# Cached grouped-query attention, twice: load gates in one table, first scores moved up, seven remainder tiles back from DMA

## The chip, the cores and the metric

The kernel runs on one core of a Trainium2 chip. The metric is device time in microseconds (us) of the whole program, from launch to the last store; lower is better. A core has a matrix engine (TensorE, PE in the profile, its weight loads PEld), a vector engine (VectorE, DVE), an activation engine (ScalarE, ACT), GpSimd (POOL) and SyncE (SP), which only issues transfers here. Transfers are issued from two in-order queues, that of SP and that of ACT, and run on 16 shared DMA engines. PSUM has eight banks, into which PE writes.

## The reference

Two independent problems, A and B, have the same shapes and are computed alike; their outputs stand side by side.

```python
B, Sq, D = 16, 80, 576
Hq, Hkv, Sk, Dh = 32, 16, 512, 128          # two query heads share one key/value head
q = (x @ wq).reshape(B, Sq, Hq, Dh).transpose(0, 2, 1, 3)
k = repeat(k_cache, 2, axis=1);  v = repeat(v_cache, 2, axis=1)
p = softmax(einsum("bhqd,bhkd->bhqk", q, k) * Dh ** -0.5)
o = einsum("bhqk,bhkd->bhqd", p, v)
out = o.transpose(0, 2, 1, 3).reshape(B, Sq, Hq * Dh) @ wo
```

All tensors are bf16. Per problem, K and V are 16 x 16 x 512 x 128 each (33.5 MB each), wq is 576 x 4096 and wo 4096 x 576.

## The kernel before

**Units.** The work is cut into 128 units (64 for A, then 64 for B). A unit is one batch and four key/value heads, so eight query heads. Its queries are 4 x 160 rows (two heads of 80 rows share a K/V head). Each 160 is split into 128 rows and 32 remainder rows; the four remainders are put together into one more tile of 128 rows. So a unit has five score tiles of 128 x 512, k = 0 for the remainders and k = 1 to 4 for the four heads. Eight units (eight batches) make an octet, with 16 octets `goct` in all. Octets come in fours: two column blocks `q` of wq for the first eight batches (`half` 0), and the same two for the last eight (`half` 1).

**A unit's steps**, with their lines in the kernel before: query projection (L581, five matmuls of 320 columns for each of eight heads and two batch groups, evicted to `qT` by ACT L592 or DVE L593); scores (L691 remainders, L705 heads); negative maximum (DVE L714); exponential with row sum (ACT L718); reciprocal (DVE L724); scaling of the probabilities (POOL L727); transposition of the probability tile into `pT` by four matmuls with the identity (PE L733) and a copy out of PSUM (DVE L739 for the remainder tile, L741 for a head's); product with V (PE L778), evicted to `oT` by ACT L794. Every 16 units, over both halves, an output projection (L831) is added into `acc` (ACT L843) or added to it and stored (DVE L859, SP L865).

**Remainder tiles by DMA.** In units that the table `RSEL` names, the remainder tile is not transposed on PE. SP issues a DMA transposition from `p_sb` to `pT` (L745), and there is no copy on DVE. `pT` has three slots (`NPT`), so the transposition of unit U may not be issued before the V products of unit U-3 are done. All four V products of unit U read what it brings. Before the change `RSEL` names 97 units.

**Loads.** SP issues, from one in-order queue: K of every unit by DMA transposition (L656, five slots), x of problem B by DMA transposition, five pieces for each half (L521), wq (L557, L554) and wo (L621) for later octets, the remainder transpositions and the output stores. V comes on ACT's queue (L660, four slots). x of A is loaded plainly (L487) and transposed on PE (L502). An issue of a K transposition can occupy SP for several microseconds.

**The planner.** The order of work is not written out. `_Sched.arrange` plays the program through with costs for each operation: each operation has a key (the step at which it is due; five steps are one unit), and where several are ready on an engine the smallest key less an `ahead` goes first. Each engine then runs the fixed order that comes out, with semaphore waits. So a constant in the planner changes the order of instructions, and is no wait by itself. `after` is a gate: a load isn't placed before a named V product (`S.marks`, four per unit) has started in the plan. `LA` = 13 lets the scores run 13 steps ahead of the V products; `lead` lets projections run 15 units ahead at first and `QL1` at the end (`QL2` for octet 1).

**Names that the change touches.** `XR`, `WQR`, `WOR`: gates of B's x, of wq and of wo, as a first unit and a step in units. `XLD`: keys of the four loads of A's x, two per half. `x` in the loop over `goct == 0`: keys of the first octet's projections, 16 of them: for each of the eight heads i one over two batches (c = 0, 160 columns) and one over six (c = 1, 480 columns); a unit's remainder scores need all eight heads of its batch. `RDO`, `PTO`, `OEO`, `OVO`: the `ahead` of the remainder transpositions, of the copies to `pT`, of the evictions to `oT`, and of those of the output projection. `QEO` is used nowhere. `VPH`, `VU0`: V of unit U from `VU0` on is gated `VPH` quarter units before its use. `NWARM2`: matmuls on dummy data while the second part of x is awaited.

Of the kernel before, what the change touches and what calls it, by code (L numbers as in the profile page):

```python
# [13 lines left out]
LA = 13  # L14
# [6 lines left out]
QL0 = 15.0  # L21
QL1 = 11.0
KC = 2.1
# [3 lines left out]
XC = 0.4  # L27
QL2 = 10.3
VC = 1.75
# [6 lines left out]
NWARM = 8  # L36
NWARM2 = 4
NWC = 4
# [5 lines left out]
VLAG = 2.0  # L44
VPH = 11
VU0 = 14
KPH = 27
# [13 lines left out]
RG = (((0, 1, 2, 3, 4),), ((0,), (1, 2, 3, 4)))  # L61
RSEL = ((18, 24, (1, 3)), (24, 46, (0, 1, 2, 3)), (46, 62, (1, 3)), (62, 126, (0, 1, 2, 3)))
RDC = 0.72
RDK = 2.0
RDO = 10.0
RDD = 1.2
PTO = 1.0
OEO = 4.0
OVO = 8.0
QEO = 6.0  # L70
RCO = 2.0
NSS = 6
OPSPLIT = 2
XLD = ((-100.0, -60.0), (-25.0, -24.9))
XH = 0.0
XB = 4.0
WQ1 = -16.8
WQ1B = 0.02
# [3 lines left out]
LPC = 29.0  # L82
WOR = (((4.0, 1.5), (12.0, 1.5)), ((9.0, 1.8), (16.5, 1.8)), ((9.0, 1.8), (16.5, 1.8)), ((9.0, 1.8), (16.5, 1.5)))
WQR = (2.0,3.5,9.5)
XR = (-12.0,1.6)

# [275 lines left out]
def bass_concat_heads__gqa_block_cached__gqa_block_cached__near_ridge_kernel(  # L362
# [27 lines left out]
    with ExitStack() as es:  # L390
# [123 lines left out]
        for half in range(NPP):  # L514
            x_ap = probs[1][0]
            st0 = UPR + 16 * half - lead[NG // 2 + 2 * half]
            for ck in range(5):
                def em_ldxt(e, x_ap=x_ap, half=half, ck=ck):
                    src = x_ap.rearrange("b s d -> (b s) d")[half * NROW:(half + 1) * NROW, :]
                    c0 = ck * 128 if ck < 4 else D - 128  # L520
                    return e.dma_start_transpose(xT[:, half, ck:ck + 1, :],  # L521
                                                 src[:, c0:c0 + 128].rearrange("n (c d) -> n c d", c=1))

                S.add("sp", 5.0 * st0 - 20.0 + 0.01 * ck, em_ldxt,
                      writes=[R(("xT", half, b_), 1) for b_ in range(NRT)] if ck == 0 else [R(("xT", half, "t", ck), 1)],
                      dsem="d_x%d0" % half, name="ldxt%d.%d" % (half, ck), stream="x", dur=0.7, cost=0.85, xp=True,
                      after=int(4 * (st0 + XR[0] + XR[1] * ck)))

# [4 lines left out]
        for goct in range(NG):  # L533
# [6 lines left out]
            for pi, (c0, c1) in enumerate(pieces):  # L540
# [10 lines left out]
                for j, (k0, k1, n0, n1) in enumerate(parts):  # L551
# [6 lines left out]

                    at = WQR[0] + WQR[1] * j if k0 == 0 else WQR[2]
                    S.add(eng, t_ld + 0.01 * k0 if goct < 2 else 5.0 * (sp_ + at), em_ldw,  # L560
# [6 lines left out]
            for i in range(8):  # L567
                for c in range(2):
                    if goct == 0:
                        b0, nb = ((0, 2), (2, 6))[c]  # L570
                        x = -LA - ((6.0, 3.6), (1.2, 0.5))[i // 4][c] + (0.6 if i < 4 else 0.05 if c == 0 else 1.2) * (i % 4)
                    else:
# [372 lines left out]
```

## Time and profile before

| | before |
|---|---|
| runs shown | 768.44, 772.54, 777.40 us; median 772.54 us |
| the profiled execution | 776.17 us, of which its span is 774.4 us |
| PE busy | 758.1 us, 98% of the span |
| DVE, ACT, POOL busy | 671.1 (87%), 608.7 (79%), 434.1 us (56%) |
| DMA moved | 173.26 MB, mean 224 GB/s; SP's queue q1 79.3%, ACT's queue q10 29.7% of 16 engines' span |
| K transpositions | 64 + 64, 512 KB each, 7.4 us from issue to landing (median) |
| V loads | 64 + 64, 512 KB each, 5.2 to 5.4 us |
| remainder transpositions | 97, 128 KB each, 5.0 us |

The 1.8 us between the profiled execution's time and its span lie outside what the profile shows of the program. The busy time of PE counts pipelined matmuls one behind the other; how far it is work is seen from the distance between starts (a 128-column matmul 56 ns, 160 columns 69 ns, 288 columns 123 ns, 320 columns 136 ns, 512 columns 216 ns apart where nothing waits). In the tables by stretch, the columns are the stretch, its length, and for each engine the busy time with the number of instructions in brackets, then the granted clock of PE, the DMA share and GB/s.

### The profile page before, as it was taken

To read this page: it belongs to the slowest core of one execution; us is meant where nothing else is said; L and a number is where in the kernel's file an instruction comes from. 1 tells how busy PE (TensorE), PEld (TensorE's weight loads), DVE (VectorE), ACT (ScalarE), POOL (GpSimd) and SP (SyncE) were. 2 spreads that over 40 slices of the span, in tenths; PEclk is the share of its full clock that TensorE was granted. 3 is DMA by queue.
4 is the path that set the end of the run, shared out by engine and by line. 5 is a ranking of instruction groups with operands and counts; after the bars stand their busy time and mean duration, and the time that the engine had idled before them with its cause. 6 is when DMAs were issued, how large, how long until landed. Compare 5 with 4: busy or idle time off the path is not lost.

```text
span 774.4 us, 20988 instructions
## 1 busy us (share of the span) xinstructions
PE 758.1 (98%) x7866; PEld 572.9 (74%) x7866; DVE 671.1 (87%) x1588; ACT 608.7 (79%) x1706; POOL 434.1 (56%) x647
## 2 busy tenths in 40 slices
PE   8999999999999997999999999999899999999998
PEld 4577777777777775777777777767677777777786
DVE  4999999888888987899899898988798988898982
ACT  1898988888888886787787878877688788888860
POOL 1565665656565655565655556665455565565650
PEclk9999999999999999999999999999999999999999
DMA  9999999999999999999999999999999999999931
GB/s 248 243 234 230 231 223 254 229 231 222 205 218 220 246 226 217 263 223 245 234 232 213 243 233 255 226 237 227 238 221 214 219 204 210 255 233 249 256 109 32
DMA packets 432996, 173.26 MB, mean 224 GB/s; under 512 B 329600, under 2 KB 432512, under 8 KB 432896
## 3 DMA queue, kind: packets, MB, share of 16 engines
q1 hardware_dynamic: 366208, 105.71, 79.3%
q10 hardware_dynamic: 66688, 66.20, 29.7%
q8 instruction: 64, 1.05, 0.6%
q14 instruction: 36, 0.29, 0.1%
HBM read 87.46 MB, written 2.95 MB: 117 GB/s over the span
## 4 chain that ended last, share of the span: by engine, by line
PE 96%; DMA 1%; ACT 1%; issue 1%; DVE 0%; SPq 0%
PE ps L581 23%; PE ps L831 20%; PE ps L778 19%; PE ps L733 16%; PE ps L705 14%; PE ps L691 4%; ACT p_sb L718 1%; DMA acc<-in_A_x_dram 1%; DMA pT<-p_sb 1%; PE ps L502 0%; DVE negmax L714 0%; ACT oT L794 0%; DVE qT L593 0%; SPq L487 0%; DVE osb L859 0%
## 5 line engine op out<-in xcount | busy, mean ns | idle before, releaser
L727 POOL TENSOR_SCALAR p_sb<-p_sb,rinv 128x512 bf16<-128x512 bf16 x640 | 431.7, 698 | 317.4 <-DVE rinv L724 317.2
L718 ACT ACTIVATE p_sb<-ps,negmax 128x512 bf16<-128x512 f32 x640 | 439.6, 693 | 60.1 <-DVE negmax L714 49.0
L714 DVE TENSOR_REDUCE negmax<-ps 128x1 f32<-128x512 f32 x640 | 424.4, 678 | 25.9 <-PE ps L691 13.5
L778 PE MATMUL ps<-pT,v_sb 128*128 128x160 bf16 x2048 | 220.9, 233 | 7.8 <-issue 5.2
L741 DVE COPY pT<-ps 128x512 bf16<-128x512 bf16 x512 | 207.9, 412 | 20.3 <-PE ps L733 17.8
L581 PE MATMUL ps<-xT,wq_sb 128*128 128x320 bf16 (+2 forms) x1280 | 213.7, 300 | 0.7 <-ACT p_sb L718 0.6
L733 PE MATMUL ps<-ident,p_sb 128*128 128x128 bf16 x2172 | 207.2, 219 | 0.0
L778 PEld LDWEIGHTS ps<-pT,v_sb 128*128 128x128 bf16 x2048 | 164.1, 98 | 54.0 <-issue 6.4
L705 PE MATMUL ps<-kT,qT 128*128 128x512 bf16 x512 | 193.9, 380 | 1.0 <-ACT p_sb L718 1.0
L733 PEld LDWEIGHTS ps<-ident,p_sb 128*128 128x128 bf16 x2172 | 154.9, 98 | 34.3 <-issue 5.9
L831 PE MATMUL ps<-wo_sb,oT 128*128 128x288 bf16 x1280 | 170.8, 286 | 0.0
L581 PEld LDWEIGHTS ps<-xT,wq_sb 128*128 128x128 bf16 x1280 | 116.8, 98 | 53.5 <-ACT oT L794 5.1
L794 ACT CAST oT<-ps 128x320 bf16<-128x320 f32 x256 | 109.1, 426 | 52.8 <-PE ps L778 50.0
L831 PEld LDWEIGHTS ps<-wo_sb,oT 128*128 128x128 bf16 x1280 | 122.8, 98 | 33.0 <-issue 0.8
L718 ACT ACTIVATION_READ_ACCUMULATOR p_sb<-ps,negmax 128x1 f32 x640 | 131.4, 205 | 0.0
L592 ACT ACTIVATE qT<-ps 128x320 bf16<-128x320 f32 (+1 forms) x129 | 56.0, 434 | 31.5 <-PE ps L581 31.1
L593 DVE TENSOR_SCALAR qT<-ps 128x320 bf16<-128x320 f32 (+2 forms) x127 | 61.7, 487 | 13.1 <-PE ps L581 12.1
L705 PEld LDWEIGHTS ps<-kT,qT 128*128 128x128 bf16 x512 | 50.1, 98 | 6.2 <-ACT p_sb L718 2.3
L859 DVE TENSOR_TENSOR osb<-ps,acc 128x288 bf16<-128x288 f32 x40 | 18.2, 456 | 29.1 <-PE ps L831 28.5
L691 PE MATMUL ps<-kT,qT 128*32 128x512 bf16 x512 | 40.0, 388 | 1.8 <-ACT p_sb L718 1.8
L724 DVE RECIPROCAL rinv<-rowsum 128x1 f32<-128x1 f32 (+2 forms) x225 | 36.7, 163 | 4.3 <-ACT p_sb L718 4.3
L843 ACT COPY acc<-ps 128x288 f32<-128x288 f32 x40 | 16.0, 399 | 4.2 <-PE ps L831 3.3
(19 smaller groups left out, 42.4 us busy)
## 6 DMA issues: line engine op xcount, KB each, us to landing
v_sb<-in_B_v_cache_dram ACTq DMA_DIRECT2D x64, 512.0 KB, 5.2
v_sb<-in_A_v_cache_dram ACTq DMA_DIRECT2D x60, 512.0 KB, 5.3
wo_sb<-in_A_wo_dram SPq DMA_DIRECT2D x16, 288.0 KB, 5.1
wo_sb<-in_B_wo_dram SPq DMA_DIRECT2D x16, 288.0 KB, 4.4
wq_sb<-in_B_wq_dram SPq DMA_DIRECT2D x16, 256.0 KB, 5.1
out_dram<-osb SPq DMA_DIRECT2D x40, 72.0 KB, 3.9
v_sb<-in_A_v_cache_dram SPq DMA_DIRECT2D x4, 512.0 KB, 5.4
wq_sb<-in_A_wq_dram SPq DMA_DIRECT2D x8, 256.0 KB, 5.1
```

The costliest lines, as they stand in the source:

```text
L581: last = e.matmul(ps[:, vb.phys, 0:n1 - n0], lhsT=wq_sb[:, wsl, ck, i * 128:(i + 1) * 128], rhs=xT[:, half, ck, n0:n1], start=(ck == 0), s ...
L593: return e.tensor_scalar(dst, src, SCALE, None, op0=AluOpType.mult)
L691: last = e.matmul(ps[32 * g4:32 * g4 + 32, vb_.phys, :], lhsT=qT[:, qp_, g4 * 160 + 128:g4 * 160 + 160], rhs=kT[:, ks_, :, g4 * 128:(g4 + ...
L705: return e.matmul(ps[:, vb.phys, :], lhsT=qT[:, qp, gl * 160:gl * 160 + 128], rhs=kT[:, ks, :, gl * 128:(gl + 1) * 128], start=True, stop= ...
L714: return e.tensor_reduce(negmax[:, si:si + 1], ps[:, vb.phys, :], axis=AX.X, op=AluOpType.max, negate=True)
L718: return e.activation(p_sb[:, psl, :], ps[:, vb.phys, :], AF.Exp, bias=negmax[:, si:si + 1], scale=1.0, accum_out=rowsum[:, ss, k:k + 1])
L727: return e.tensor_scalar(p_sb[:, psl, :], p_sb[:, psl, :], rinv[:, ss, k:k + 1], 1.0, op0=AluOpType.mult, op1=AluOpType.mult)
L733: last = e.transpose(psb[:, vt.phys, j * 128:(j + 1) * 128], p_sb[:, psl, j * 128:(j + 1) * 128], ident[:])
L741: return e.tensor_copy(pT[:, pts, :, 0:4, gl * 32:gl * 32 + 32], psb[:, vt.phys, 0:512].rearrange("p (j h c) -> p j h c", j=4, h=4))
L778: last = e.matmul(ps[:, vo.phys, off:off + 160], lhsT=v_sb[:, vs, gl, j * 128:(j + 1) * 128], rhs=pT[:, pts, j, :, gl * 32:gl * 32 + 32], ...
L794: return e.copy(dst, src)
L831: last = e.matmul(ps[:, vb.phys, 0:DC], lhsT=oT[:, hi, rb * 128:(rb + 1) * 128], rhs=wo_sb[:, hi, c3 * DC:(c3 + 1) * DC], start=(hi == 0), ...
```

## The change

The loads of wq, wo and B's x get gates of their own by half and by column block, so that they are spread further apart: B's first x half comes over units 36 to 40 (before 38.75 to 45), its second over 57.75 to 64.5 (before 55.25 to 61.75). The second half of A's x is loaded after the first four K tiles, not ahead of all. In the first octet, two of the eight projections over six batches come before the first scores, not four, and the other six are given keys between those of the scores. In units 78 to 91 only every second remainder tile goes by DMA, so that 90 do in all; seven more go by PE and DVE. Some priorities, V's gate (a quarter of a unit later, and from unit 10 on) and the number of dummy matmuls are changed with it. No instruction computes anything else.

```diff
-QL1 = 11.0
+QL1 = 10.5
-QL2 = 10.3
+QL2 = 10.6
-NWARM2 = 4
+NWARM2 = 2
-VPH = 11
-VU0 = 14
+VPH = 10
+VU0 = 10
-RSEL = ((18, 24, (1, 3)), (24, 46, (0, 1, 2, 3)), (46, 62, (1, 3)), (62, 126, (0, 1, 2, 3)))
+RSEL = ((18, 24, (1, 3)), (24, 46, (0, 1, 2, 3)), (46, 62, (1, 3)), (62, 78, (0, 1, 2, 3)), (78, 92, (1, 3)), (92, 126, (0, 1, 2, 3)))
-RDO = 10.0
+RDO = 6.0
-PTO = 1.0
-OEO = 4.0
-OVO = 8.0
-QEO = 6.0
+PTO = 2.0
+OEO = 8.0
+OVO = 0.0
+QEO = 0.0
-XLD = ((-100.0, -60.0), (-25.0, -24.9))
+XLD = ((-100.0, -60.0), (-8.0, -7.9))
+G0H = -2.9
+G0C = (-3.6, -3.2, 1.2, 2.7, 4.2, 5.7, 7.2, 8.2)
-WOR = (((4.0, 1.5), (12.0, 1.5)), ((9.0, 1.8), (16.5, 1.8)), ((9.0, 1.8), (16.5, 1.8)), ((9.0, 1.8), (16.5, 1.5)))
-WQR = (2.0,3.5,9.5)
-XR = (-12.0,1.6)
+WOR = (((4.0, 1.5), (12.0, 1.5)), ((9.0, 2.0), (17.0, 2.0)), ((9.0, 2.0), (17.0, 2.0)), ((9.0, 2.0), (17.0, 1.5)))
+WQR = ((2.0, 2.5, 11.0), (4.0, 2.5, 12.0))
+XR = ((-14.8, 0.9), (-10.0, 1.7))
...
-                      after=int(4 * (st0 + XR[0] + XR[1] * ck)))
+                      after=int(4 * (st0 + XR[half][0] + XR[half][1] * ck)))
...
-                    at = WQR[0] + WQR[1] * j if k0 == 0 else WQR[2]
+                    at = WQR[q % 2][0] + WQR[q % 2][1] * j if k0 == 0 else WQR[q % 2][2]
...
-                        x = -LA - ((6.0, 3.6), (1.2, 0.5))[i // 4][c] + (0.6 if i < 4 else 0.05 if c == 0 else 1.2) * (i % 4)
+                        x = -LA + (G0C[i] if c else -6.0 + 0.6 * i if i < 4 else G0H + 0.05 * (i - 4))
```

## The prediction

> **What bounds the kernel now.** I read the page first: the busy shares, the slices, the chain. Then the busy times by stretches of 20 us, SP's own timeline where PE falls short, and the chain there.
>
> ```profile
> PE 758.1 (98%) x7866; PEld 572.9 (74%) x7866; DVE 671.1 (87%) x1588; ACT 608.7 (79%) x1706; POOL 434.1 (56%) x647
> PE 96%; DMA 1%; ACT 1%; issue 1%; DVE 0%; SPq 0%
> ```
>
> PE is busy 98% of the span and carries 96% of the chain that ended last. So time is gained only by giving PE less to do or by taking away its few holes. The stretches show them:
>
> ```profile
> 0.00:20.00 20.00, 17.53 (x125) 9.95 (x126) 10.31 (x23) 3.75 (x8) 2.44 (x7) 1.00 1.02 248
> 20.00:40.00 20.00, 18.43 (x181) 11.82 (x179) 19.57 (x45) 17.07 (x48) 10.98 (x17) 1.00 1.06 251
> 40.00:60.00 20.00, 20.00 (x215) 15.04 (x213) 18.99 (x44) 18.02 (x51) 12.63 (x19) 1.00 1.14 234
> 300.00:320.00 20.00, 15.41 (x148) 11.20 (x146) 13.94 (x33) 12.95 (x36) 8.81 (x14) 0.91 1.23 219
> 500.00:520.00 20.00, 18.65 (x192) 13.66 (x190) 17.42 (x40) 16.52 (x49) 10.86 (x17) 1.00 1.16 225
> 520.00:540.00 20.00, 19.36 (x202) 14.94 (x201) 16.99 (x41) 14.60 (x42) 10.82 (x17) 1.00 1.09 234
> 540.00:560.00 20.00, 16.93 (x175) 12.46 (x173) 14.24 (x34) 13.37 (x38) 10.09 (x16) 1.00 1.08 230
> ```
>
> PE, the first busy time, is full from 40 us to the end, apart from two places: 300 to 320 us (4.59 us short, and its clock mean only 0.91) and 500 to 560 us (1.35, 0.64 and 3.07 us short). The start is the third place. What ends the holes is seen in the timelines of SP and PE and, for the later place, in the chain (start, length, what):
>
> ```profile
> 297.66 3.34 SPq L656 DMA_TRANSPOSE kT<-in_A_k_cache_dram  x1
> 301.10 1.22 SPq L745 DMA_TRANSPOSE pT<-p_sb  x1
> 307.76 0.44 PE L778 MATMUL ps<-pT,v_sb 128*128 128x160 bf16 x4 [4.59 <-issue]
> ...
> 541.96 4.84 DMA pT<-p_sb
> 546.85 0.45 PE ps L778 x4
> ```
>
> PE's first hole ends at the V product of unit 49. The waits call this one "issue", but by the landing records that unit's remainder transposition, issued at 301.10, landed at 307.67. Its slot had been free since 292.72, the end of unit 46's last V product. So it stood 8.4 us behind other issues, of which the K transposition from 297.66 was the last, and left the V product 0.09 us of slack. I made the same three numbers for all 97 transpositions. From unit 24 to 44 the lag is 0 to 2.6 us and the slack 6 to 11 us. It then rises to 11.5 us at unit 51, and again from 2.2 us at unit 80 to 9 at unit 84 and 12 at unit 90; units 49, 84, 86, 87 and 89 have slack under 0.25 us, and those are the holes. A lag of about 8.4 us is where PE begins to pay.
>
> **The change, part by part.** The sum goes against the profiled execution: 776.17 us, that is 774.4 of span and 1.8 around it. It lies 3.6 us above the median of the runs shown, whose holes I take to be smaller by about that.
>
> (1) *The holes, and their price.* PE short 4.59 + 1.35 + 0.64 + 3.07 = 9.65 us. The first one also costs clock: the clock records give half speed from 308.4 to 311.8 us, which loses 1.7 us. Together 11.35 us. The shorter holes left the clock at 1.00.
>
> (2) *Do the new gates empty the queue there?* I added up the bytes whose gate lies in a span of units (K and V 1.05 MB a unit, remainder 0.131, wo piece 0.295, wq piece 0.262 and 0.131, x piece 0.164). Units 41 to 50: 14 loads before, 9 after; 13.8 MB against 12.75. At 10 units of 5.6 us less what the hole takes, about 50 us, that is 275 against 255 GB/s, where the stretches with a backlog moved 219 to 250. Units 36 to 41 take up what was moved: 3 loads before, 7 after, 6.5 against 7.2 MB in 28.7 us, 226 against 252 GB/s. Measured lag before grew by 10 us where my excess makes 6, so I scale by 1.7: after the change about 1.5 us at unit 41 and 5 to 6 at unit 50, under 8.4. Units 78 to 84: before 8.75, after 8.2 MB (three remainders fewer); units 84 to 90: 8.3 against 7.9. A lag of 4 to 5 us instead of 9 to 12. Units 84 and 86 have no transposition left to wait for. So both places clear, by 3 us of lag. I leave 1.5 us for small waits: **-9.85 us**. Ends: all 11.35 gone, or half (5.7).
>
> (3) *Seven remainder tiles on PE.* 7 x 4 matmuls x 56 ns = **+1.57 us**, all on the path, since PE is full there. Seven copies of 410 ns (L739) are 2.9 us of DVE, beside PE: DVE has 1.5 to 3 us free in each 20 us from 500 on and 1.15 from 480 to 500; there two copies use 0.8 of it. SP loses seven issues of 1.2 us.
>
> (4) *The start.* PE runs without a hole from 8.27 to the first scores:
>
> ```profile
> 8.27 7.99 PE L581 MATMUL ps<-xT,wq_sb 128*128 128x160 bf16 x65
> 16.19 0.40 PE L691 MATMUL ps<-kT,qT 128*32 128x512 bf16 x4
> 17.59 0.69 ACT L718 ACTIVATE p_sb<-ps,negmax 128x512 bf16<-128x512 f32 x1 [3.04 <-DVE negmax L714]
> 23.22 0.39 PE L705 MATMUL ps<-kT,qT 128*128 128x512 bf16 x1 [0.40 <-ACT p_sb L718]
> ```
>
> Two projections of five 480-column matmuls (1.01 us each) leave the road to the first scores: they come 2.0 us earlier. They need the second wq piece (landed 11.5 us) and K of unit 0 (12.94); both gain from two x loads leaving the queue ahead of them. From 20 to 31 us PE has holes of 0.3 to 0.7 us because ACT frees score banks too slowly (the last line); an earlier start of ACT fills them with the projections put off. What limits it: DVE is 19.57 of 20 busy from 20 to 40 us, and K of unit 5 landed at 35.23 for scores at 37.09, a slack of 1.86 that bytes, not order, decide. So the gain is at most 2.5 and I take **-1.5 us**. The other side: the second half of A's x, landed at 8.8 and 11.4 us before, now comes behind K of unit 3 and, by the K and V landings (25.18, 27.82, 29.21), at about 24 and 28 us. PE transposed it from 26.8 to 32 us, so up to 1 us earlier would now wait; at worst +1.5. The Trainium skill's "DMA: Bandwidth & Descriptors", section "Rules for kernel authors", says to issue a transfer early and wait for it late, which speaks against this move; by it the start would lose that 1.5 us and the sum be 769.4; no row of before can show it.
>
> (5) *V's gate* is a quarter unit, 1.1 to 1.6 us, later. V's slack at its product is 4 us and more except at units 15, 82 and 83 (2.8, 3.1, 2.5 us), so 0; with cover gone, some 1 us at each. *Dummy matmuls*: two fewer (0.43 us) lie in a wait for x (1.2 us), 0. *Priorities*: an op eviction that waits behind one exponential (0.69 us) holds one of the two banks that projections share with V products; PE has other work ready, 0, bounds -1 and +2. *RDO* lets a wq issue (0.58 us) go ahead of a remainder; beside 3 us of room, 0. *Lead* of projections: 0, the same matmuls.
>
> Sum: 776.17 - 9.85 + 1.57 - 1.5 = **766.4 us**, 0.8% under the median. One per cent (7.7 us: 764.8 and 780.3) is about what a measurement of this kernel tells from no change, for its runs spread by 9 us.
>
> **Rivals.**
> - *Everything clears* (chance 0.25): no hole is left and the start gives its full 2.5: 776.17 - 11.35 + 1.57 - 2.5 = 763.9. For it: at units 62 to 78 and 92 to 126, with every remainder by DMA, no wait of PE shows. Against it: DVE's 19.57.
> - *Half the holes stay* (0.2): the loads are moved and no byte but 0.92 MB is saved; 252 GB/s at units 36 to 41 already exceeds what backlogged stretches moved. 776.17 - 5.7 + 1.57 = 772.0, no change against the median.
> - *Remainders late all over* (0.1, slower): with `RDO` 6 each wq, wo or K that is ready passes a remainder in SP's order, and with five x pieces in under four units, at a place where every unit has one, the lag passes 8.4 us before unit 46. The two old places keep their holes and a third of the first one's price (4.59 + 1.7) is added; 776.17 + 6.3 + 1.57 - 1.5 = 782.5. Against it: lag 0 to 1.1 us at units 34 to 43 before, with two x pieces among them.
> - *The forecast* (0.45).
>
> The range goes from just under the first rival to above the third case, whose small start loss it takes in: 763 to 775. Faster by over 1%: the first rival and a sixth of the forecast, 0.32; slower 0.1; within 1% 0.58.
>
> **What would show it.** PE full in 300 to 320 and 500 to 560 us with clock 1.00; remainder transpositions issued within 6 us of their slot's release at units 45 to 55 and 80 to 92; first remainder scores near 14 us; L733 x2200. Wrong if a hole of over 2 us stands before a V product (L778), or if PE waits between 24 and 33 us for the transposition of x (L502), or if a stretch after 40 us falls short with DVE over 19.5.

## The result

| | before | after |
|---|---|---|
| median of 20 runs | 773.92 us (766.92 to 793.91) | 779.15 us (773.05 to 785.67) |
| ratio to before, 95% interval | 1 | 1.0102 [1.0071, 1.0132] |
| profiled execution, its span | 776.17, 774.4 us | 776.12, 774.4 us |
| PE's work at full rate | 738.0 us | 739.1 us |
| PE's loss against it | 32.3 us | 31.1 us |

The forecast was 766.4 us, 0.8% faster; by the ratio the changed kernel is 1.0% slower. The two profiled executions take the same time, so the traces tell what was traded, and only the comparisons tell which way the sum leans. Ratios are taken over runs within 1.5% of the fastest run of the same kernel, here 18 of 20 against 14 of 20, so a ratio can differ from the quotient of two medians (1.007 here). *Work* and *loss* come from the distances between the starts of neighbouring matmuls: the work is the distance where nothing waits (56 ns for 128 columns and so on), the loss is the rest. About 0.4 us in each 20 us of loss is there in every stretch.

The page of the changed kernel: the busy line, the chain's shares by engine, and the group of the transpositions on PE.

```profile
PE 759.6 (98%) x7892; PEld 573.3 (74%) x7892; DVE 677.6 (88%) x1594; ACT 607.2 (78%) x1700; POOL 434.1 (56%) x647
PE 86%; DMA 6%; DVE 5%; SPq 2%; ACT 1%; issue 0%; ACTq 0%
L735 PE MATMUL ps<-ident,p_sb 128*128 128x128 bf16 x2200 | 209.1, 219 | 0.3 <-DVE pT L743 0.2
```

PE is as full as before, with 28 more transposition matmuls. The chain is another: 6% of it is now DMA (1% before) and 2% SP's queue. (The 5% of DVE stand for no hole: the chain of `e_light`, below, has 4% and PE is full.) The stretches of the changed kernel, columns as before:

```profile
0.00:20.00 20.00, 16.21 (x112) 9.17 (x113) 9.29 (x22) 4.61 (x10) 2.44 (x7) 1.00 1.03 217
20.00:40.00 20.00, 19.78 (x188) 12.95 (x186) 18.85 (x41) 16.26 (x46) 10.12 (x15) 1.00 1.12 249
300.00:320.00 20.00, 18.65 (x198) 13.64 (x196) 18.58 (x45) 16.36 (x45) 12.19 (x19) 1.00 1.21 248
340.00:360.00 20.00, 17.62 (x190) 13.30 (x188) 15.63 (x38) 13.41 (x39) 10.91 (x17) 1.00 1.08 248
460.00:480.00 20.00, 18.77 (x200) 14.16 (x198) 16.74 (x39) 15.42 (x43) 11.17 (x17) 1.00 1.16 250
500.00:520.00 20.00, 20.00 (x209) 15.09 (x207) 17.85 (x42) 16.75 (x49) 12.72 (x20) 1.00 1.12 241
520.00:540.00 20.00, 20.00 (x211) 15.60 (x210) 17.63 (x43) 15.75 (x43) 10.94 (x17) 1.00 1.04 247
540.00:560.00 20.00, 20.00 (x214) 14.98 (x213) 17.41 (x42) 17.25 (x49) 12.76 (x20) 1.00 1.25 195
720.00:740.00 20.00, 18.89 (x203) 14.38 (x201) 18.11 (x44) 15.96 (x45) 12.44 (x20) 1.00 1.13 227
```

Three of these stretches had been full in the kernel before:

```profile
340.00:360.00 20.00, 20.00 (x210) 15.34 (x209) 17.92 (x43) 16.22 (x45) 11.69 (x18) 1.00 1.22 246
460.00:480.00 20.00, 20.00 (x213) 15.26 (x211) 17.93 (x44) 16.92 (x48) 13.17 (x20) 1.00 1.14 234
720.00:740.00 20.00, 20.00 (x221) 15.52 (x218) 19.49 (x48) 17.07 (x48) 13.37 (x21) 1.00 1.10 233
```

The holes that the prediction wanted filled are nearly filled: 500 to 560 us is full, and 300 to 320 us is 1.35 us short at clock 1.00, where it was 4.59 short at 0.91. New holes stand elsewhere. In loss of PE, half clock included:

| stretch | before | after | difference |
|---|---|---|---|
| 300 to 320 and 500 to 560 us | 13.25 | 3.50 | -9.75 |
| 340 to 360 | 0.42 | 2.95 | +2.53 |
| 440 to 500 | 1.28 | 4.06 | +2.78 |
| 560 to 580 | 0.20 | 1.28 | +1.08 |
| 720 to 740 | 0.41 | 1.65 | +1.24 |
| 0 to 40 (start) | 6.31 | 7.11 | +0.80 |
| the rest | 10.45 | 10.59 | +0.14 |

Together -1.18 us; with 1.13 us more work (seven remainder tiles 1.57, two dummy matmuls -0.43) that is -0.05 us, the difference of the two profiled times. So 7.8 us of holes at new places, after 40 us, have eaten most of what the old places gave. But the profiled execution of before lies 2.3 us over the median of its runs, and that of after 3 us under: a mean run of the changed kernel loses 3.6 us at half clock (mean granted clock 0.995 over 20 runs), its profiled execution none between 6.9 and 774.9 us.

What ends the largest new hole is read from the chain of the changed kernel (start, length, what):

```profile
347.34 4.03 SPq L658
351.37 0.05 issue
351.42 5.19 DMA wo_sb<-in_A_wo_dram
356.61 0.14 issue
356.74 2.12 PE ps L833 x16
```

The last piece of wo for the output projection was issued at 351.42, behind a K transposition whose issue held SP for 4 us, landed at 356.61, and the projection (L833) started 0.13 us later. In the kernel before the same piece had landed 7.64 us before it was wanted. PE's waits in the changed kernel (for what, us in total, times, longest) put this wait first:

```profile
PE ps L833 <- DMA wo_sb<-in_A_wo_dram: 2.8, 2, 2.4
PE ps L780 <- DMA pT<-p_sb: 2.4, 3, 1.2
PE ps L504 <- DMA acc<-in_A_x_dram: 1.8, 1, 1.8
```

The second line is the remainders, whose transpositions are still late at unit 49 and newly at 51, 73, 76 and 92 (slack 0.13 us each). Their lag behind the release of their slot, which the prediction saw falling to 4 to 6 us, has a mean of 3.2 us over all units (2.9 before), and 21 units have over 6 us (16 before). At units 73, 76 and 92 the lag was only 3.3, 4.5 and 4.6 us; there the transfer itself was slow, 7.8 to 8.6 us from issue to landing against a median of 5.1.

### The profile page after: what moved, and what is told of

The parts are those of the page before. It is cut to its first block, busy times and chain, and to the rows that moved or that the text cites. A ratio compares the mean times of both kernels' runs of the same rounds, so it can differ in the third digit from the quotient of the medians.

```text
span 774.4 us, 21004 instructions
## 1 busy us (share of the span) xinstructions
PE 759.6 (98%) x7892; PEld 573.3 (74%) x7892; DVE 677.6 (88%) x1594; ACT 607.2 (78%) x1700; POOL 434.1 (56%) x647
## 2 busy tenths in 40 slices
DMA packets 429188, 172.34 MB, mean 223 GB/s; under 512 B 325792, under 2 KB 428704, under 8 KB 429088
## 3 DMA queue, kind: packets, MB, share of 16 engines
HBM read 87.46 MB, written 2.95 MB: 117 GB/s over the span
## 4 chain that ended last, share of the span: by engine, by line
PE 86%; DMA 6%; DVE 5%; SPq 2%; ACT 1%; issue 0%; ACTq 0%
PE ps L583 20%; PE ps L833 19%; PE ps L780 16%; PE ps L735 14%; PE ps L707 13%; PE ps L693 4%; DMA pT<-p_sb 3%; DVE negmax L716 3%; SPq L658 2%; DMA wo_sb<-in_A_wo_dram 1%; DVE pT L743 1%; DMA wq_sb<-in_A_wq_dram 1%; ACT p_sb L720 0%; DVE pT L741 0%; SPq L559 0%
## 5 line engine op out<-in xcount | busy, mean ns | idle before, releaser
L716 DVE TENSOR_REDUCE negmax<-ps 128x1 f32<-128x512 f32 x640 | 423.5, 680 | 22.3 <-PE ps L707 11.6
L735 PEld LDWEIGHTS ps<-ident,p_sb 128*128 128x128 bf16 x2200 | 156.5, 98 | 37.3 <-DVE pT L743 5.9
L833 PE MATMUL ps<-wo_sb,oT 128*128 128x288 bf16 x1280 | 171.0, 286 | 2.8 <-DMA wo_sb<-in_A_wo_dram 2.8
L833 PEld LDWEIGHTS ps<-wo_sb,oT 128*128 128x128 bf16 x1280 | 122.5, 98 | 38.9 <-DVE rinv L726 2.6
L594 ACT ACTIVATE qT<-ps 128x320 bf16<-128x320 f32 (+2 forms) x123 | 53.8, 437 | 33.4 <-PE ps L583 32.3
L595 DVE TENSOR_SCALAR qT<-ps 128x320 bf16<-128x320 f32 (+2 forms) x133 | 64.6, 486 | 14.3 <-PE ps L583 12.5
```

The lines of the kernel that those rows point to most:

```text
L595: return e.tensor_scalar(dst, src, SCALE, None, op0=AluOpType.mult)
L716: return e.tensor_reduce(negmax[:, si:si + 1], ps[:, vb.phys, :], axis=AX.X, op=AluOpType.max, negate=True)
L735: last = e.transpose(psb[:, vt.phys, j * 128:(j + 1) * 128], p_sb[:, psl, j * 128:(j + 1) * 128], ident[:])
L833: last = e.matmul(ps[:, vb.phys, 0:DC], lhsT=oT[:, hi, rb * 128:(rb + 1) * 128], rhs=wo_sb[:, hi, c3 * DC:(c3 + 1) * DC], start=(hi == 0), ...
```

## Experiments

Three theories stood at first: the **gates** (new places for the loads make other loads late), the **start** (the first scores are not earlier), and the **remainder tiles** (seven more on PE). Later came the **wo wait** and the **priorities**. "Undone" means the changed kernel with the values of before; "alone" means the kernel before with the new values.

| kernel | what | median (range), us | before beside it | ratio [95%] |
|---|---|---|---|---|
| `after2` | the change again | 775.74 (766.94 to 785.09) | 773.40 | 1.0032 [0.9988, 1.0075] |
| `e_light` | the change, lighter wq and wo loads | 767.86 (766.66 to 773.30) | 773.40 | 0.9973 [0.9935, 1.0011] |
| `u_gates` | gates of x, wq, wo undone | 772.95 (769.20 to 782.45) | 772.82 | 1.0007 [0.9975, 1.0039] |
| `u_x` | gates of x undone | 773.56 (770.69 to 779.85) | 777.62 | 1.0008 [0.9968, 1.0049] |
| `u_w` | gates of wq, wo undone | 772.05 (768.07 to 781.50) | 777.62 | 0.9965 [0.9922, 1.0009] |
| `u_w2` | `u_w` again | 774.83 (767.90 to 783.74) | 773.41 | 1.0037 [0.9999, 1.0075] |
| `u_gv` | all gates and V's undone | 780.15 (772.39 to 798.52) | 777.62 | 1.0079 [1.0030, 1.0127] |
| `d_gates` | gates of x, wq, wo alone | 784.01 (772.21 to 792.26) | 777.62 | 1.0062 [1.0003, 1.0122] |
| `u_vgate` | V's gate undone | 776.81 (770.09 to 786.23) | 772.82 | 1.0049 [1.0017, 1.0082] |
| `u_rsel` | 97 remainders by DMA | 778.44 (772.24 to 795.85) | 772.82 | 1.0075 [1.0028, 1.0122] |
| `d_rsel` | 90 remainders, alone | 773.55 (766.24 to 783.22) | 773.40 | 1.0007 [0.9963, 1.0050] |
| `d_xr` | x gates and 90 remainders, alone | 771.80 (766.45 to 778.42) | 773.41 | 0.9987 [0.9946, 1.0027] |
| `u_start` | start undone | 782.23 (766.74 to 795.75) | 772.82 | 0.9999 [0.9934, 1.0063] |
| `u_ws` | gates of wq, wo and x loads of the start undone | 774.17 (770.33 to 781.49) | 773.40 | 1.0029 [0.9991, 1.0067] |
| `u_wo` | gates of wo undone | 775.10 (769.15 to 784.11) | 773.41 | 1.0025 [0.9989, 1.0061] |
| `x_wo` | gates of wo later still | 776.82 (769.12 to 783.28) | 773.41 | 1.0058 [1.0023, 1.0094] |
| `u_pri` | the five priorities undone | 773.33 (768.60 to 782.02) | 776.05 | 0.9998 [0.9953, 1.0044] |
| `d_pri` | the five priorities alone | 778.34 (774.77 to 785.91) | 776.05 | 1.0110 [1.0026, 1.0194] |

### The change again

No edit; it tells how far one comparison carries.

> The changed kernel once more, on the same chip as the next three. 0.4 to 1.0% over the kernel before; if it is level with it here, the loss lies within what chips differ by and the load gates are not its cause.

It came out 0.3% slower, with an interval that takes in no change, against 1.0% in the first comparison; the intervals overlap only from 0.71 to 0.75%. So the forecast gain of 0.8% is ruled out, the cost is put at 0.3 to 1.0%, and a difference of 0.7% between two of the kernels below, compared at different times, is not to be read by itself. The trace has the wait for wo at the same place, longer, and this time it costs clock as well (stretches of `after2`):

```profile
340.00:360.00 20.00, 16.96 (x180) 12.60 (x178) 16.07 (x38) 14.02 (x41) 12.73 (x19) 0.96 1.22 234
360.00:380.00 20.00, 20.00 (x189) 14.93 (x188) 15.54 (x37) 11.37 (x33) 7.38 (x11) 0.87 1.01 198
```

PE's gap before the output projection is 3.20 us, and the clock is at half from 358.3 to 365.1 us: 3.4 us more. One wait of this kind, 6.6 us in all, is 0.85% of the run.

Of the new holes of the first trace, this is the only one that the second repeats: the loss is 1.28 us at 440 to 500 us, 0.43 at 560 to 580 and 0.59 at 720 to 740, as before the change or near it, and only 6 remainders lag over 6 us (21 in the first trace). The sum does repeat: the two old places give 10.1 us, 8.1 us are lost at other places after 40 us (6.0 of it at 340 to 380 us) and 1.0 more at the start. So a part of the places in one trace is chance, and that something is lost elsewhere is not.

### Is it the load on the DMA engines?

```diff
+                        if wv > 1:
+                            return e.dma_start(wq_sb[:, wsl, k0:k0 + 1, n0:n1], src[0:128, :].rearrange("(c p) n -> p c n", p=128))
...
+                    if sg:
+                        return e.dma_start(wo_sb[:, wc * hc:wc * hc + 1, c3 * DC:(c3 + 1) * DC],
+                                           src[0:128, :].rearrange("(h p) n -> p h n", p=128))
```

> The changed kernel, but of every later wq and wo piece (third weight block on) only a quarter of its rows is loaded: 10 MB of 173 less, with the same issues at the same places; the rest of the weights is stale, so the output is another. If late remainder transpositions and K tiles behind a full queue make all of PE's holes after the start: holes gone between units 36 and 110, lag under 3 us, 764 to 767 us and runs within 6 us. If the order of the issues on SP (one behind a K that blocks) makes them and not the bytes: 773 us or more.

Of every later wq and wo piece only a quarter is loaded, so that the kernel leaves out a part of the weights and its output is another. With 10 of 172 MB less and every instruction kept, the holes go. Stretches of `e_light`:

```profile
300.00:320.00 20.00, 20.00 (x214) 14.98 (x212) 19.84 (x47) 17.43 (x49) 12.65 (x19) 1.00 1.07 236
340.00:360.00 20.00, 20.00 (x216) 15.32 (x209) 18.09 (x44) 14.47 (x41) 10.12 (x16) 1.00 0.96 201
500.00:520.00 20.00, 20.00 (x216) 15.11 (x215) 17.50 (x42) 16.43 (x47) 11.59 (x18) 1.00 1.00 201
540.00:560.00 20.00, 20.00 (x212) 15.53 (x214) 16.70 (x40) 16.64 (x49) 12.28 (x19) 1.00 0.99 200
```

PE is full at the DMA's 200 to 236 GB/s, where the changed kernel moves 195 to 248 there. No remainder lags over 6 us (mean 0.9), and after 40 us no hole is over 0.4 us. Its median is 7.9 us under that of `after2` on the same chip. So the holes of the changed kernel are loads that come late because too much is to be moved, and those 10 MB decide. The same kernel's runs spread over 6.6 us, those of `after2` over 18: the spread, too, is mostly made by the transfers. The kernel before was not run with the lighter loads, so this tells what makes the holes, and not what makes the changed kernel slower than the kernel before.

### The gates

`u_gates` (`u_x` has the second line alone, `u_w` and `u_w2` the first and third):

```diff
-WOR = (((4.0, 1.5), (12.0, 1.5)), ((9.0, 2.0), (17.0, 2.0)), ((9.0, 2.0), (17.0, 2.0)), ((9.0, 2.0), (17.0, 1.5)))
+WOR = (((4.0, 1.5), (12.0, 1.5)), ((9.0, 1.8), (16.5, 1.8)), ((9.0, 1.8), (16.5, 1.8)), ((9.0, 1.8), (16.5, 1.5)))
-XR = ((-14.8, 0.9), (-10.0, 1.7))
+XR = ((-12.0, 1.6), (-12.0, 1.6))
-WQR = ((2.0, 2.5, 11.0), (4.0, 2.5, 12.0))
+WQR = ((2.0, 3.5, 9.5), (2.0, 3.5, 9.5))
```

> The changed kernel with the load gates of before (B's x, wq, wo). Theory G: the backlog at units 64 to 82 goes (lag of the remainder transpositions there back to 0 to 3 us from 4 to 8), the one at 45 to 57 stays; 773 to 775 us. Theory V and theory S: the lag at 64 to 82 stays 4 us or more, and the time 778 us or more.

> The changed kernel with only the gates of B's x as before. All engines but SP keep their order; on SP the ten x pieces move. Theory Gx, that five x pieces in four units, where every unit has a remainder transposition, start the backlog: 773 to 775 us, and the slack of the remainder transpositions at units 41 to 45 back from a mean of 3.7 to 6 us or more. Theory Gw, that the wq and wo pieces, now issued in pairs behind one K, do it: 778 to 780, slack at 41 to 45 under 5 us.

> The changed kernel with only the gates of wq and wo as before. Theory Gw: 773 to 775 us. Theory Gx: 778 to 780 us, slack at units 41 to 45 under 5 us.

> Once more the changed kernel with the wq and wo gates of before, whose first result was 0.4% under the kernel before with an interval that takes in no change. If that was real: 0.2 to 0.6% faster again. If chance: level or slower.

With the gates of before, all or a part of them, the changed kernel is level with the kernel before. The lag that was expected to go with `u_gates` didn't: at units 64 to 82 its mean is 5.5 us (5.4 in the changed kernel). That `u_w` seemed 0.35% faster is not borne out: the second comparison of the same kernel gives 0.4% slower. In its second trace there is no hole at unit 49, but one of 5.21 us at 150 us, where K is late, and one of 1.67 at 532: the queue falls behind somewhere, and not always in the same place.

The hole at unit 49 follows the gates as predicted. With the old gates of x, wq and wo it is 4.76 us (before), 4.79 (`d_rsel`), 4.29 (`u_gates`), 3.38 (`u_gv`) and more in `d_pri` (below); with the new ones 1.02 (after), 1.17 (`after2`), 1.27 (`u_start`), 1.29 (`u_rsel`), and there is none in `u_vgate`, `u_pri` and `d_gates`. That piece of the mechanism is shown.

```diff
 # u_gv: the three lines of u_gates, and
-VPH = 10
-VU0 = 10
+VPH = 11
+VU0 = 14
```

> The changed kernel with the load gates and V's gate as before; new start, 90 remainders by DMA and priorities stay. If the two gates are all that costs: 768 to 771 us, under the kernel before, with no hole of over 3 us in the units 78 to 92. If V's gate does nothing beside the load gates: 772 to 774, as with the load gates alone undone.

```diff
 # d_gates: the kernel before with
+WOR = (((4.0, 1.5), (12.0, 1.5)), ((9.0, 2.0), (17.0, 2.0)), ((9.0, 2.0), (17.0, 2.0)), ((9.0, 2.0), (17.0, 1.5)))
+WQR = ((2.0, 2.5, 11.0), (4.0, 2.5, 12.0))
+XR = ((-14.8, 0.9), (-10.0, 1.7))
```

> The kernel before with only the new load gates (B's x, wq, wo). Theory G: 5 to 7 us over the kernel before, 777 to 780. If the gates cost only together with V's later gate or with the new start: within 2 us of the kernel before.

`u_gv` missed both times that were expected, and the two runs speak against one simple cause. `u_gv` has no new gate at all and is still 0.8% slower: by this time, something in what is left (start, seven tiles, priorities) costs. `d_gates` has only the gates and is 0.6% slower, with the interval ending at 0.0%: by this time, the gates cost as well. `u_gates` and `u_gv` differ in V's gate alone and are 0.7% apart, with intervals that meet between 1.0030 and 1.0039. The parts don't add up; but two comparisons of one kernel lay as far apart, so neither time is proof of a cost of its own.

```diff
 # u_vgate
-VPH = 10
-VU0 = 10
+VPH = 11
+VU0 = 14
```

> The changed kernel with V gated as before (11 quarter units ahead, from unit 14 on). Theory V: lag of the remainder transpositions at units 64 to 100 halves, and 772 to 775 us. Theories G and S: 778 to 780 us, lag as in the changed kernel.

V's gate undone alone: 0.5% slower than before, between the two comparisons of the change. No wait for V shows on PE with the new gate; the mean slack of V at its product falls from 8.4 us to 7.7. No cost of it is shown.

### The remainder tiles

```diff
 # u_rsel: the changed kernel with (d_rsel: the other way round, in the kernel before)
-RSEL = ((18, 24, (1, 3)), (24, 46, (0, 1, 2, 3)), (46, 62, (1, 3)), (62, 78, (0, 1, 2, 3)), (78, 92, (1, 3)), (92, 126, (0, 1, 2, 3)))
+RSEL = ((18, 24, (1, 3)), (24, 46, (0, 1, 2, 3)), (46, 62, (1, 3)), (62, 126, (0, 1, 2, 3)))
```

> The changed kernel with the 97 remainder transpositions of before. PE does 1.6 us less. Theories G and V (the queue is the bound of units 78 to 92): the lag there grows from 6 to 8 us to 10 to 13 and the time goes to 780 to 784 us. If PE's added work is what made the change slower, 777.5 us.

> The kernel before with only the seven remainder tiles of units 78 to 91 moved from DMA to PE. PE does 1.6 us more. By the prediction's second step the holes at units 84 to 89 (5 us in the profile before) go: 0.3 to 0.5% faster. If the backlog there comes from K and V and stays, or moves on: 0 to 0.4% slower.

Alone, the seven tiles are worth nothing that shows, either way. `u_rsel` missed its expectation: the lag at units 78 to 92 is 4.3 us, and not 10 to 13. In the trace of `d_rsel` 500 to 560 us is full, the hole at 303.6 us stays (4.79 us, and 6.8 us of half clock), and its time is level with before (stretches of `d_rsel`):

```profile
300.00:320.00 20.00, 15.38 (x142) 11.15 (x140) 13.25 (x32) 11.93 (x35) 7.40 (x11) 0.83 1.13 219
540.00:560.00 20.00, 20.00 (x214) 15.08 (x212) 17.49 (x43) 15.67 (x44) 13.25 (x20) 1.00 1.05 215
```

So in this trace the holes at 500 to 560 us go when these seven transpositions leave the queue; 1.57 us of the gain are paid on PE, and the other 3.5 us (0.45%), which the prediction counted, don't show in the runs. That the seven tiles decide there is not shown: `d_pri` keeps them on DMA and is 0.32 us short in these 60 us, and `u_gv` has them on PE and loses 7.45 us there.

```diff
 # d_xr: the kernel before with
+RSEL = ((18, 24, (1, 3)), (24, 46, (0, 1, 2, 3)), (46, 62, (1, 3)), (62, 78, (0, 1, 2, 3)), (78, 92, (1, 3)), (92, 126, (0, 1, 2, 3)))
+XR = ((-14.8, 0.9), (-10.0, 1.7))
```

> The kernel before with the new gates of B's x and 90 remainders alone: the parts that no run so far has shown to cost anything, without the new wo and wq gates and the new start. A candidate under both kernels: 0.3 to 0.8% faster than before, by holes at 303 and 512 to 546 us of less than half. If the holes move whatever is done: level with the kernel before.

The two parts that empty the two old places, without the others: 0.1% faster, not told apart from no change, where 0.3 to 0.8% was expected. The hole at 303.6 us is halved, to 2.44 us. By the ratio only `u_w` came out lower, once of two times.

### The start

```diff
 # u_start
-QL2 = 10.6
+QL2 = 10.3
-NWARM2 = 2
+NWARM2 = 4
-XLD = ((-100.0, -60.0), (-8.0, -7.9))
+XLD = ((-100.0, -60.0), (-25.0, -24.9))
-                        x = -LA + (G0C[i] if c else -6.0 + 0.6 * i if i < 4 else G0H + 0.05 * (i - 4))
+                        x = -LA - ((6.0, 3.6), (1.2, 0.5))[i // 4][c] + (0.6 if i < 4 else 0.05 if c == 0 else 1.2) * (i % 4)
```

> The changed kernel with the start as it was before (keys of the first octet's projections, of the loads of A's second x half, dummy matmuls, key of octet 1). Theory G, that the moved load gates carried the backlog of SP's queue to units 42 to 51 and 64 to 82: no better, 777 to 780 us, since the backlog lies far behind the start. Theory V, that V's gate a quarter unit later makes V run beside K and holds up SP's queue: the same 777 to 780. Theory S, that the start costs what is lost (PE's loss in the first 40 us went from 8.9 to 9.3 us, and V and K then run in another order): 774 to 776.

The times tell little: two of the 12 runs took 766.7 and 771 us and the others 778 to 796. They show no gain from the old start. The traces tell more. PE's start in the changed kernel:

```profile
8.54 1.00 PE L504 MATMUL ps<-ident,acc 128*128 128x128 bf16 x15 [1.78 <-DMA acc<-in_A_x_dram]
9.37 6.25 PE L583 MATMUL ps<-xT,wq_sb 128*128 128x160 bf16 x55
15.55 0.40 PE L693 MATMUL ps<-kT,qT 128*32 128x512 bf16 x4
```

The first projection begins at 9.37 us (8.27 before) and the first remainder scores at 15.55 (16.19 before; 14.2 predicted). The second part of the first x half now lands at 8.40 us (7.30 before) with K of unit 0 right behind it, and that K lands at 13.32 (12.94 before): taking two x loads out of the queue brought neither forward. With the two loads back (`u_ws`, below) that part of x lands at 7.52 us. In the 13 other traces that have the new order of the first octet the first scores stand between 15.02 and 18.28 us, in the six with the old order between 16.19 and 16.87. The V product of unit 10 starts at 85.0 us (85.7 before). What the new order wins in two projections it pays in the wait for x and, in nine of those 14 traces, in 3.4 us or more of half clock between 7.5 and 14.4 us, which no trace with the old order has.

```diff
 # u_ws: the values of before for WOR, WQR, XLD and NWARM2; the new keys of the first octet stay
-XLD = ((-100.0, -60.0), (-8.0, -7.9))
+XLD = ((-100.0, -60.0), (-25.0, -24.9))
```

> The changed kernel with the gates of wq and wo, the loads of A's second x half and the four dummy matmuls as before; B's x gates, keys of the first scores, 90 remainders, V's gate and priorities stay. First projection back at 8.3 us from 9.2 to 10.2 and no half clock at 8 to 12 us. If the start theory holds (the x load that the first projections need shares the engines with K of unit 0): 1 to 2.5 us under the kernel with the wq and wo gates alone undone, 0.6 to 0.9% under the kernel before. Else level with it, 0 to 0.4% under.

With the x loads where they were, the new keys bring the first projection to 8.49 us and the first scores to 15.02; but then a hole of 2.95 us follows at 15.6 us and half clock from 18.9 to 22.3. The time, 0.3% over before, shows no gain.

### The wait for wo

```diff
 # u_wo
-WOR = (((4.0, 1.5), (12.0, 1.5)), ((9.0, 2.0), (17.0, 2.0)), ((9.0, 2.0), (17.0, 2.0)), ((9.0, 2.0), (17.0, 1.5)))
+WOR = (((4.0, 1.5), (12.0, 1.5)), ((9.0, 1.8), (16.5, 1.8)), ((9.0, 1.8), (16.5, 1.8)), ((9.0, 1.8), (16.5, 1.5)))
```

> The changed kernel with only the gates of wo as before (steps of 1.8 from 9 and 16.5). Theory W, that the later wo gates bring the last wo piece of a block to the output projection too late: no wait of PE before an output projection at 355 and 545 us (2.5 to 3.2 us and 0.2 to 1 us with the new gates), slack of the last piece over 1 us at all four places, 2 to 4 us under the changed kernel. Theory B, that the backlog of remainder transpositions alone counts: the same holes move before V products, time as the changed kernel.

```diff
 # x_wo
-WOR = (((4.0, 1.5), (12.0, 1.5)), ((9.0, 2.0), (17.0, 2.0)), ((9.0, 2.0), (17.0, 2.0)), ((9.0, 2.0), (17.0, 1.5)))
+WOR = (((4.0, 1.5), (12.0, 1.5)), ((9.0, 2.0), (18.0, 2.0)), ((9.0, 2.0), (18.0, 2.0)), ((9.0, 2.0), (17.0, 1.5)))
```

> The changed kernel with the second wo block of the two middle output projections gated one unit (about 6 us) later still. Theory W: the waits before the output projection at about 355 and 545 us grow by 3 to 6 us each, to 5 to 9 and 3 to 6, with half a clock for 3.4 us or more behind them; 784 us or more. Theory B: the queue is emptier where remainders are late, so level with or below the changed kernel.

`u_wo` shows the wait's cause. In the ten kernels profiled with the old gates of wo the last piece of a block lands 0.33 us or more, mostly 2 to 13, ahead of the matmuls that need it, and PE has no gap there. Of those with the gates of the change, `e_light` apart, each of the eight has at least one place where these matmuls start 0.13 us behind the last piece, at the cost of 0.4 to 3.8 us (3.8 in `d_gates`, traced in its longest run, 792.26 us). Undoing these gates takes the wait away, but the time only from +0.3 to +1.0% to +0.25%, which the intervals don't separate.

`x_wo` missed its expectation. Gates one unit later didn't make the wait one unit longer: the planner saw the load coming later and put the projection at 362.1 us in place of 356.7, with 4.92 us of slack. The wait of the change stands where the planner believed that the piece was in time, and the chip's queue was slower than its costs. The 0.6% of `x_wo` stay without a cause: the traced run, its shortest (769.12 us), has no hole of PE over 1.4 us after 40 us.

### The priorities

```diff
 # u_pri (d_pri: the other way round, in the kernel before)
-RDO = 6.0
-PTO = 2.0
-OEO = 8.0
-OVO = 0.0
+RDO = 10.0
+PTO = 1.0
+OEO = 4.0
+OVO = 8.0
```

> The changed kernel with the five priorities of before (RDO 10, PTO 1, OEO 4, OVO 8, QEO 6); gates, start, remainder choice stay. If the priorities take a part of the loss of their own, this goes to 0 to +0.4% of the kernel before (0.4% or more under the changed kernel's two comparisons of +0.3 and +1.0%). If they cost nothing, as the prediction held (step 5), it stays at +0.3 to +1.0%. The wait before the output projection (0.13 us after the last wo piece) should stay, since the wo gates do.

> The kernel before with the five new priorities alone. If the priorities cost, +0.3 to +0.6% against the kernel before; if they cost nothing, within 0.3% of it, with the holes before the V product near 303 us (4 to 5 us) and at 500 to 560 us still there, and no wait for wo before the output projection.

Undone, the change is level with before; alone, the priorities make the kernel before 1.1% slower by the ratio. That rests on six runs with an interval 1.7% wide, and the medians say 0.3%; and `u_pri` and `after2` have intervals that overlap. So a cost of the priorities is possible, and neither it nor its size is shown. What they can do is seen in the trace of `d_pri`, on SP's queue at unit 49:

```profile
298.54 3.74 SPq L656 DMA_TRANSPOSE kT<-in_A_k_cache_dram  x1
302.32 0.58 SPq L557 DMA_DIRECT2D wq_sb<-in_B_wq_dram  x1
303.00 3.09 SPq L745 DMA_TRANSPOSE pT<-p_sb  x1
306.13 6.13 SPq L656 DMA_TRANSPOSE kT<-in_A_k_cache_dram  x1
```

In the kernel before, SP issued unit 49's remainder ahead of the wq piece:

```profile
301.10 1.22 SPq L745 DMA_TRANSPOSE pT<-p_sb  x1
302.36 0.58 SPq L557 DMA_DIRECT2D wq_sb<-in_B_wq_dram  x1
```

Now the piece goes first. The remainder's issue takes 3.09 us in place of 1.22, it lands 9.7 us after its issue (6.6 before), at 312.70, and the V product starts at 312.79 (307.76 before). The gaps on PE there are 6.4 and 2.3 us, and 10.2 us of half clock follow (PE, then the stretch):

```profile
309.99 1.04 PE L691 MATMUL ps<-kT,qT 128*32 128x512 bf16 x8 [6.23 <-issue]
312.79 0.69 PE L778 MATMUL ps<-pT,v_sb 128*128 128x160 bf16 x4 [1.76 <-issue]
300.00:320.00 20.00, 12.01 (x107) 8.49 (x104) 9.74 (x24) 8.83 (x25) 6.45 (x10) 0.74 1.10 188
```

Only the second gap ends with the remainder. The first and longer one ends at scores that now stand ahead of that V product in PE's order, 0.09 us after K of unit 53 landed, at 309.90 us (307.44 before); that K was issued at 298.54, ahead of the wq piece. So the passed remainder is shown, and that the whole hole comes from it is not.

PE is 7.99 us short in that stretch (4.59 before). With the old priorities in the changed kernel, both old places are full (stretches of `u_pri`):

```profile
300.00:320.00 20.00, 20.00 (x220) 15.16 (x219) 19.63 (x48) 18.36 (x53) 13.12 (x21) 1.00 1.18 238
340.00:360.00 20.00, 17.27 (x180) 12.75 (x178) 15.79 (x38) 13.87 (x39) 12.11 (x18) 0.98 1.22 264
500.00:520.00 20.00, 20.00 (x213) 15.19 (x210) 18.11 (x43) 17.26 (x49) 11.91 (x18) 1.00 1.19 270
540.00:560.00 20.00, 20.00 (x212) 15.06 (x211) 17.52 (x43) 16.67 (x47) 12.59 (x20) 1.00 1.03 224
```

Only two of its remainders lag over 6 us (21 and 6 in the two traces of the changed kernel). What it keeps is the wait for wo, as its chain shows:

```profile
353.25 4.96 DMA wo_sb<-in_A_wo_dram
358.22 0.14 issue
358.35 3.30 PE ps L833 x16
```

2.90 us of gap and 3.4 us of half clock, 4.6 us together, and at the start a loss of 9.6 us to 40 us (6.3 before). In this trace that takes back most of what the filled holes give. The lag alone doesn't prove the priorities guilty: kernels with the new ones range from none (`e_light`) or 1 to 24 units over 6 us.

**Not tried:** `QL1` alone; the kernel before with the lighter loads; the change with old priorities, old wo gates and old start together. By the trace of `u_pri` (774.92 us, 4.6 for wo and 3.3 at the start) the latter would be an estimate of 767 us, which no run bears out. How the 0.3 to 1.0% divide between gates, priorities and start stays open: the parts don't add up, and two comparisons of one kernel differ by as much as the parts do.

## Why the prediction was wrong, point by point

- **The sum.** The profiled execution took 776.12 us, 9.7 us over the forecast. Of these, 7.8 us are holes at places that the sum didn't contain (2), and 2.3 us are the start (4); 0.4 us of work less than forecast goes the other way. `after2` has the same shape: 8.1 us at other places.
- **What bounds the kernel** held: PE is 98% busy, and most of the loss is in holes that transfers make. But three places were read as *the* holes. The first stands in all five traces with the old gates of x, wq and wo; the later one comes and goes between traces.
- **(1) The holes' price** (9.65 us and 1.7 of clock) was read rightly; but a mean run of before seems not to hold all of it. `d_rsel` fills 500 to 560 us and is no faster. Nor was the first hole the remainder's alone: K of unit 53, which the next scores in PE's order wait for, landed at 307.44 us, 0.23 us before it, so by these times the remainder alone, brought earlier, would have moved most of that hole by half a microsecond.
- **(2) "So both places clear"** came out almost to the number: -9.85 predicted, -9.75 measured (-10.1 in `after2`). The step failed in what it left out: new holes elsewhere stood in the sum at nothing, and were 7.8 us. It added up the bytes of the stretches that lose loads, and of one stretch that takes them up (units 36 to 41); it didn't ask where else the queue has no room. The lag at units 62 to 78 rose from 2.8 to 4.8 us (2.4 in `after2`), and the remainders came late at 73, 76 and 92. "Issued within 6 us" was wrong at units 47 to 55 (6.2 to 8.5 us) and for the mean of units 78 to 92 (6.4; 1.9 in `after2`). Nor is a lag of 8.4 us where PE begins to pay: units 73, 76 and 92 paid at 3.3 to 4.6, because their transfers took long, and unit 51 of the kernel before had 11.5 with 3.8 us of slack.
- **The later gate of wo was never priced.** The bytes of each wo piece were counted, its deadline wasn't. wo is loaded in two blocks of four pieces for each of the four output projections (one for 32 units); in the two middle projections the second block's pieces come half a unit later at the first and 1.25 units (7 us) at the last one. The slack before was 1.0 and 7.6 us at the two blocks of the first of these projections, 6.0 and 0.33 at the second. That view was at hand: 7 us out of 7.6 leave no room for a late queue. The wait that followed was 2.5 us (6.6 with clock in `after2`); `u_wo` shows that it goes with these gates.
- **(3) Seven tiles, +1.57 us**: the 28 matmuls are there and PE's work grew by just that; the DVE copies hid.
- **(4) Start, -1.5 us**: +0.8 in the profile. The limiting term was the landing of the second part of the first x half and of K of unit 0, which were taken to gain from the shorter queue and came 1.1 and 0.4 us later. The bound that was named (second x half late, +1.5) didn't come: PE has one gap between 24 and 33 us, 0.22 us, and it waits there for a copy into `pT`. The Trainium skill's rule in "DMA: Bandwidth & Descriptors", "Rules for kernel authors" (issue early, wait late) had the sign by luck: the loss stands in the first half of x, and not in the loads that were issued later, so no run here bears the rule out.
- **(5) The priorities at 0, and `RDO` at 0 "beside 3 us of room"** is not borne out, and its price is open: by the ratios 1.1% alone and 0.3 to 1.0% back when undone, by the medians 0.3% alone. The room didn't exist at unit 49 of the kernel before, whose slack of 0.09 us the prediction itself quoted; passed by the wq piece, that remainder landed 5.0 us later. V's gate and the dummy matmuls at 0: no wait for V appeared; the two fewer dummy matmuls lie in a wait for x that grew from 1.2 to 1.8 us, and the half clock that follows in most traces was not foreseen.
- **Rivals.** "Remainders late all over" (chance 0.1) named a way of loss that `d_pri` shows (`RDO` lets loads pass a remainder), but kept the two old holes, which went, and set the new place before unit 46. "Half the holes stay" (0.2) was right that bytes which are only moved are late elsewhere, and wrong about the place. The changed kernel has neither the hole of over 2 us before a V product, nor the wait for x at 24 to 33 us, nor a short stretch with DVE over 19.5 (18.1 at 720 to 740 us) that would have told it wrong: its largest hole stands before another instruction, the output projection.

## What to carry to other kernels

When a transfer queue is nearly full, a hole that is filled can come up elsewhere: before counting it as won, find where the moved load lands and who waits for it there, deadline by deadline, for every gate that changes. A priority that lets one issue pass another is free only where the one passed has slack, so price it at the unit with the least, not at the mean. Compare the profiled execution with the spread of runs before a hole's whole price goes into the sum, and try parts both ways, undone and alone, and one kernel twice, since parts that share a queue need not add up.

## What the runs showed of the hardware

- **How full the transfers were.** The changed kernel moves 172.34 MB at a mean of 223 GB/s, and single stretches of 20 us reach 270 (`u_pri`, 500 to 520 us). At that load the 12 to 35 runs of one kernel spread by 9 to 29 us; with 6% fewer bytes (162.31 MB, 212 GB/s) by 6.6 us.
- **An issue can take long, and holds what stands behind it.** The same remainder issue held SP 1.22 us in one order and 3.09 us in the other; K transpositions of 512 KB held it 2.8 to 6.7 us around 300 us (before), and everything behind them in SP's queue stood as long.
- **Half clock after short gaps.** The clock record falls to half for 3.4 us after gaps of 2.15 us (`u_x` at 304.8, half from 308.0), 2.44 (`d_xr` at 303.6, half from 307.4) and 2.4 to 2.95 at the start, and not after 2.54 us (the changed kernel at 354.1), 2.83 (`u_start` at 353.5) and 3.21 (`u_rsel` at 355.2). After 3.20 us (`after2`) it lasted 6.8 us and after 6.4 and 2.3 us (`d_pri`) 10.2. So in this range a gap's length alone doesn't tell whether it costs clock. The Trainium skill's "TensorE: Matmul & The Clock Gate", section "Part 1: The HAM clock gate", says that the clock drops after an idle window of about 3.4 us, and that the window runs freely. The steps of 3.4 us agree; that gaps a third shorter than a window already cost one doesn't follow from it.
